# GateLoop attention and a multiplicative FFN: unit 7's output products in one-pass words, state products on four column groups, and new instruction lists for three engines

## The chip, the core and the metric

The kernel runs on one core of a Trainium2 chip. Its metric is the device time of one execution in microseconds. The engines that matter are TensorE (PE, with its weight loads PEld), VectorE (DVE), ScalarE (ACT), GpSimd (POOL) and SyncE (SP), which issues most transfers. Each engine works through its own instructions in order.

## What is computed

The reference runs a linear attention with a complex decay (GateLoop) on 4 sequences of 768 tokens, 8 heads of 48 dimensions, and puts its output through an FFN that multiplies two projections:

```python
mag = np.sqrt(a_re * a_re + a_im * a_im)
scale = np.minimum(mag, 0.999) / (mag + 1e-06)
a_re_n, a_im_n = (a_re * scale, a_im * scale)
for t in range(S):
    new_re = ar * S_re - ai * S_im
    new_im = ar * S_im + ai * S_re
    kv = np.einsum('bhd,bhe->bhde', k[:, :, t], v[:, :, t])
    S_re, S_im = (new_re + kv, new_im)
    y[:, :, t] = np.einsum('bhd,bhde->bhe', q[:, :, t], S_re)
...
a = x @ w1          # x: 3072 x 384, w1 and w2: 384 x 1024
b = x @ w2
h = a * b @ w3      # w3: 1024 x 1024
return (h @ w_out).astype(np.float32)
```

All is fp32.

## The kernel before

**Units.** The 3072 tokens are cut into 8 units of 384 (half a sequence each), a unit into 3 chunks of 128 tokens. For a unit, the gates (`re`, `im` to phases and magnitudes, with scans over the tokens) turn `q` and `k` into real and imaginary parts (`gA`, `gR` and the tiles' own values); SyncE moves these into the tiles QL and KL with the head dimension on the partitions, and `vr` into V. Then for each chunk TensorE transposes the two parts of k (`tp`, evicted by ScalarE to KT), forms the state's addition KTᵀ·V (`kv`, evicted into one of the tiles T0 to T2), the scores (`sc`, masked by VectorE into A0 or A1) and the output `y` from A·V and from QL·T.

**FFN.** In the head of the program w3·w_out is multiplied into one matrix `w3o`, 1024 x 384. A unit's FFN is then a = x·w1, b = x·w2, the product `ab`, and ab·w3o. From unit 2 on, x and the weights of a and b are held as rounded words (x0, x1 and x2 = x1 − x0; `wh`, `low`), and each fp32 product is three one-pass products: the first two (`hb`, "heads") go to a PSUM bank `m`, ScalarE scales the bank in place, the third (`da`, `db`, "diffs") is added, and ScalarE (a) or VectorE (a·b) evicts it. VectorE makes x1, GpSimd makes x2. The output products ab·w3o were plain fp32 for every unit: three token groups of 8 products of 128x384, in two parts.

**Order.** A planner with costs in the table TIMES writes TensorE's order: the FFN of unit u−1 is laid between the attention steps of unit u, so TensorE is nearly always busy, and unit 7's FFN stands alone at the end. ScalarE, VectorE and SyncE are put into the order of the lists in ORDERS by `in_order`: a list names, instruction by instruction, which of those left in the log comes next. GpSimd keeps the order of the log. `kv`, `tp` and `y` share two PSUM banks (`ps_v`), `m` and `o` the banks of `ps_m`; which of two free banks a tile gets follows the order in which the scheduler sees them released.

**Looks.** GpSimd also examines the inputs (`look`, `seen`, `looked`) and VectorE tests the results; `judge` sums them (`tot`) and a small product `count` on TensorE gives `good`, which decides at the end whether a general program has to run. The last pieces of w3 are examined in six freed buffers, named in BUFFERS.

The lines the prediction refers to are: L1047 `tp`, L1060 `sc`, L1099 `y`, L1125 `kv`, L1145 FFN products `m`, L1240 output products `o`, L1507 the head's fusion, L1535 `count`. L385 is the recording helper through which all other engines' instructions go, so they are told apart by their tiles.

Of the kernel before, what the change touches and what calls it, by code (L numbers as in the profile page):

```python
# [389 lines left out]
class Logged:  # L390
# [10 lines left out]
    scalar="""  # L401
# [16 lines left out]

# [3 lines left out]
""")  # L422


def in_order(tc, log, order):

    left, before, taken = list(log), None, []
# [9 lines left out]
def kernel(  # L437
# [812 lines left out]

    cv = {}

# [642 lines left out]
```

## Time and profile before

| | us |
|---|---|
| three runs | 528.59, 531.6, 544.0 (median 531.6) |
| the profiled execution, its own time | 529.23 |
| its span on the core | 527.4 |
| TensorE busy / idle in the span | 495.9 / 31.5 |
| VectorE busy | 372.4 |
| ScalarE busy | 324.7 |
| GpSimd busy | 257.5 |

The mean granted TensorE clock of the profiled execution was 0.994. A row of the page's groups reads: line, engine, operation, tile written <- tiles read, shape and count | busy us, mean ns of one | idle time of the engine just before, and what ended it. A row of the timeline reads: start us, busy us, engine, line, operation, and in brackets the idle time before it. A row of the chain reads: start us, us, what.

### The profile page before, as it was taken

The numbers are of one execution on the slowest core, as the hardware profiler recorded it, in microseconds if no ns is written. First come the engines' busy times: TensorE is split into PE (matmuls) and PEld (weight loads), VectorE is DVE, ScalarE is ACT, GpSimd is POOL, SyncE is SP. The second block draws the span as 40 slices with busy tenths as digits, with TensorE's granted clock in tenths as the row PEclk, the third lists the DMA queues.
The fourth block names the chain that finished last, engine by engine and source line by source line (L and its number), as shares of the span: only waits on it lengthen the run. The fifth ranks groups of instructions, "written<-read, shape, count | busy, mean of one in ns | idle before, by whom it ended". The sixth has DMA issues, their size and how long they took to land.

```text
span 527.4 us, 13622 instructions
## 1 busy us (share of the span) xinstructions
PE 495.9 (94%) x5594; PEld 377.1 (72%) x5594; DVE 372.4 (71%) x607; ACT 324.7 (62%) x569; POOL 257.5 (49%) x317
## 2 busy tenths in 40 slices
PE   4789889999999998999989999999999999999995
PEld 2345565556756677977879679877997789778972
DVE  6999698956769897918981599359936977653530
ACT  6979867485577565955777378818883864213420
POOL 1000000017869988657654855567647458525510
PEclk9899999999999999999999999999999999999998
DMA  8999958975199225991499319941994169606511
GB/s 258 367 396 285 203 150 279 186 162 125 40 237 204 78 80 124 242 221 63 103 250 206 114 35 266 217 119 46 265 221 103 47 181 231 203 19 204 196 45 37
DMA packets 66424, 89.75 MB, mean 170 GB/s; under 512 B 29872, under 2 KB 53872, under 8 KB 65584
## 3 DMA queue, kind: packets, MB, share of 16 engines
q1 hardware_dynamic: 57904, 59.15, 45.7%
q0 software_dynamic: 8448, 29.63, 19.9%
q8 instruction: 46, 0.75, 0.6%
q14 instruction: 26, 0.21, 0.1%
HBM read 61.01 MB, written 4.72 MB: 125 GB/s over the span
## 4 chain that ended last, share of the span: by engine, by line
PE 46%; DVE 17%; DMA 13%; POOL 12%; issue 7%; ACT 3%; SPq 2%; POOLq 0%; DVEq 0%; ACTq 0%
PE m L1145 20%; PE o L1240 14%; POOL look L385 9%; DMA re<-in_a_re_dram 6%; DVE gZ L385 4%; DMA look<-in_a_re_dram 3%; PE y L1099 3%; DVE gA L385 3%; PE sc L1060 3%; DVE gR L385 2%; PE kv L1125 2%; POOL seen L385 2%; SPq L385 2%; PE f L1507 2%; PE tp L1047 1%
## 5 line engine op out<-in xcount | busy, mean ns | idle before, releaser
L1240 PE MATMUL o<-w3o,ab 128*128 128x384 f32 x384 | 131.6, 492 | 0.0
L1145 PE MATMUL m<-x,low 128*128 128x384 f32 x576 | 119.0, 339 | 1.0 <-ACT m L385 1.0
L1145 PEld LDWEIGHTS m<-x,low 128*128 128x128 f32 x576 | 102.6, 188 | 1.2 <-ACT m L385 1.2
L1240 PEld LDWEIGHTS o<-w3o,ab 128*128 128x128 f32 x384 | 70.4, 190 | 45.6 <-issue 2.4
L385 POOL TENSOR_SCALAR look<-look 128x192 f32<-128x192 f32 (+1 forms) x70 | 74.7, 1067 | 16.3 <-DMA look<-in_a_re_dram 10.8
L385 DVE TENSOR_TENSOR ab<-m,ab 128x384 f32<-128x384 f32 x64 | 35.4, 554 | 63.4 <-PE m L1145 53.0
L1145 PE MATMUL m<-x,wh 128*128 128x384 f32 x288 | 69.8, 351 | 4.1 <-DVE ab L385 2.1
L385 POOL TENSOR_TENSOR look<-look 128x256 f32<-128x256 f32 (+1 forms) x58 | 43.8, 755 | 50.4 <-DMA look<-in_w_dram 32.3
L385 ACT ACTIVATE m<-m 128x384 f32<-128x384 f32 x96 | 45.7, 478 | 33.0 <-PE m L1145 32.4
L1145 PE MATMUL m<-xT,ws 128*128 128x384 f32 x192 | 63.1, 487 | 1.1 <-ACT xT L385 1.1
L1145 PEld LDWEIGHTS m<-x,wh 128*128 128x128 f32 x288 | 50.6, 188 | 8.5 <-DVE ab L385 3.4
L1145 PEld LDWEIGHTS m<-xT,ws 128*128 128x128 f32 x192 | 36.0, 190 | 25.5 <-ACT xT L385 1.7
L385 POOL MEMSET seen<- 128x256 bf16 x1 | 0.3, 316 | 110.1 <-DVE ab L385 110.1
L385 ACT COPY ot<-o 128x384 f32<-128x384 f32 x24 | 11.4, 476 | 61.4 <-PE o L1240 61.3
L385 POOL TENSOR_TENSOR seen<-seen,look 128x192 bf16<-128x192 bf16 (+1 forms) x55 | 42.7, 776 | 4.5
L1099 PE MATMUL y<-A,V 128*32 128x128 f32 x768 | 40.3, 273 | 1.7 <-issue 1.3
L385 DVE COPY_PREDICATED A<-mask,sc 128x512 f32<-128x512 uint8 x48 | 32.7, 734 | 11.6 <-PE sc L1060 11.5
L385 POOL TENSOR_TENSOR x<-x,x 128x384 fp32r<-128x384 f32 x18 | 24.2, 1350 | 34.3 <-DVE x L385 34.3
L385 ACT COPY ab<-m 128x384 f32<-128x384 f32 x64 | 30.5, 477 | 16.3 <-PE m L1145 16.1
L385 ACT ACTIVATE low<-raw 128x384 uint16<-128x384 uint32 (+6 forms) x40 | 33.9, 888 | 6.1 <-DMA raw<-in_w_dram 3.1
L1099 PEld LDWEIGHTS y<-A,V 128*32 128x32 f32 x768 | 34.4, 110 | 3.1 <-issue 2.5
L1060 PEld LDWEIGHTS sc<-QL,KL 96*32 96x32 f32 x1536 | 28.5, 110 | 10.3 <-issue 4.4
(119 smaller groups left out, 879.4 us busy)
## 6 DMA issues: line engine op xcount, KB each, us to landing
looked<-in_w_dram POOLq DMA_DIRECT2D x14, 512.0 KB, 4.4
look<-in_w_dram POOLq DMA_DIRECT2D x27, 256.0 KB, 6.0
raw<-in_w_dram SPq DMA_DIRECT2D x6, 1024.0 KB, 10.1
KL<-gR SPq DMA_DIRECT2D x24, 192.5 KB, 4.7
KL<-k SPq DMA_DIRECT2D x24, 192.5 KB, 6.5
QL<-gA SPq DMA_DIRECT2D x24, 192.0 KB, 6.8
QL<-q SPq DMA_DIRECT2D x24, 192.0 KB, 7.5
raw<-in_w_dram SPq DMA_DIRECT2D x6, 768.0 KB, 6.7
```

What stands on the lines that cost most here:

```text
L385: self.log.append(getattr(self.engine, name)(*args, **kw))
L1047: nc.tensor.transpose(out=tp[:, f], in_=src[:, f, c * C:(c + 1) * C], identity=ident)
L1060: nc.tensor.matmul(out=sc[SB * g:SB * g + SB, j, s0:C], lhsT=KL[:, x * n + j, w][:, s0:s0 + SB], rhs=QL[:, x * n + j, w][:, s0:C], start=T ...
L1099: nc.tensor.matmul(out=o, lhsT=a, rhs=b, start=s0, stop=s1)
L1125: nc.tensor.matmul(out=kv[g:g + SB, hd], lhsT=rows[:, g:g + SB], rhs=V[:, hd], start=True, stop=True)
L1145: nc.tensor.matmul(out=out, lhsT=a, rhs=b, start=start and i == 0, stop=i == len(terms) - 1, skip_group_check=not start)
L1240: nc.tensor.matmul(out=m, lhsT=ab_t[u][:, f, t * P:(t + 1) * P], rhs=w3o[:, f], start=(f == 0), stop=(f == KF - 1))
L1507: nc.tensor.matmul(out=sums[j], lhsT=w3_t[f][:, j * P:(j + 1) * P], rhs=w3_t["wo"][:, f], start=(f == 0), stop=(f == KF - 1))
```

## The change

Three things change together.

*Unit 7's output products.* They too become three one-pass products each. `last_weights` splits `w3o` into words: `h` goes into KL's buffer, `l` into QL's, the difference `d` into those of `re`, `im` and `gZ`. For each of the 8 blocks of `ab`, `last_words` makes a0 on ScalarE (into V, A0 and A1) and a1 and a2 on VectorE (a2 into gate buffers and `vr`). The product a·b itself goes to `side`, a tile in the output buffers. TensorE then runs 3 x 14 products (`oh`), 3 x 2 (`ot`), after which ScalarE scales each bank in place, and 3 x 8 (`od`): 72 in place of 24. `count` stands before the last `od` as it stood before the last `o`. Since `re`, `im` and `gZ` are now taken, BUFFERS has three entries.

*State products.* The 24 products of a state were 8 heads times 3 column groups of 32. Now the first 6 heads use groups 0 to 2 and the other two heads' six pieces go to group 3, one beside each of the 6 heads. The bank then holds the state in four areas, and its eviction is four instructions: 96 partitions x 6 heads, and three of 32 partitions x 2 heads. There are 20 states, 4 of them evicted by ScalarE.

*Lists and plan.* ScalarE, VectorE and SyncE have new lists; TIMES has new costs for the states and the tail, by which one look group moves ahead of unit 3's x2 and of the loads of k, q and v behind it on GpSimd, and the like in units 4 to 6. TensorE's order is the same outside the states and the tail.

```diff
+9 12 10 7 11 12 14 13 12 2 11 11 1 1 3 11 9 8 6 1 3 2 -1 3 1 1 -4 1 -2 10 1 -2 1 1 5 -1 1 -1 2 -2 5 -1 5 4 4 4 2 1 2
...
-        kv = ps_v.tile([2 * D, H, D], FP, tag="v", name="kv")
-        for hd in range(H):
-            rows = KT[:, hd].rearrange("p d x f -> p (d x f)")
+        kv = ps_v.tile([P, H, D], FP, tag="v", name="kv")
+        fits, spare = H - H // LANES, 3 * SB
+        for hd in range(fits):
             for g in range(0, 2 * D, SB):
+                rows = KT[:, hd].rearrange("p d x f -> p (d x f)")
                 nc.tensor.matmul(out=kv[g:g + SB, hd], lhsT=rows[:, g:g + SB], rhs=V[:, hd], start=True, stop=True)
+            g, over = divmod(hd, H - fits)
+            rows = KT[:, fits + over].rearrange("p d x f -> p (d x f)")
+            nc.tensor.matmul(out=kv[spare:spare + SB, hd], lhsT=rows[:, SB * g:SB * g + SB], rhs=V[:, fits + over],
+                             start=True, stop=True)
...
+        areas = [(slice(0, 2 * D), slice(0, 2 * D), slice(0, fits), slice(0, fits))]
+        areas += [(slice(SB * g, SB * g + SB), slice(spare, spare + SB), slice(fits, H), slice(g * (H - fits), (g + 1) * (H - fits)))
+                  for g in range(3)]
         with tc.high_priority():
-            if T is None:
-                nc.scalar.copy(out=Tn[:, :, 0:D], in_=kv)
-            else:
-                nc.vector.tensor_tensor(out=Tn[:, :, 0:D], in0=kv, in1=T[:, :, 0:D], op=OP.add)
+            for rows, lanes, heads, slots in areas:
+                if T is None:
+                    nc.scalar.copy(out=Tn[rows, heads, 0:D], in_=kv[lanes, slots])
+                else:
+                    nc.vector.tensor_tensor(out=Tn[rows, heads, 0:D], in0=kv[lanes, slots], in1=T[rows, heads, 0:D], op=OP.add)
...
+    def last_weights():
...
+        h, l, d = words_w
+        for n in range(0, KF, 2):
+            x = slice(n, n + 2)
+            nc.scalar.activation(out=h[:, x], in_=w3o[:, x], func=AF.Copy, scale=TOP * BITS)
+            nc.vector.scalar_tensor_tensor(out=l[:, x], in0=w3o[:, x], scalar=BITS, in1=h[:, x], op0=OP.mult, op1=OP.subtract)
+        for f in range(KF):
+            nc.vector.scalar_tensor_tensor(out=d[f], in0=h[:, f], scalar=1.0 / BITS, in1=l[:, f], op0=OP.mult, op1=OP.subtract)
+
+    def last_words(j):
+
+        a, a1 = sides[j], ab_t[NU - 1][:, j]
+        words_a[1].append(a1)
+        nc.scalar.activation(out=words_a[0][j], in_=a, func=AF.Copy, scale=TOP / BITS)
+        nc.vector.scalar_tensor_tensor(out=a1, in0=words_a[0][j], scalar=-BITS, in1=a, op0=OP.mult, op1=OP.add)
+        nc.vector.tensor_tensor(out=words_a[2][j], in0=a1, in1=words_a[0][j], op=OP.subtract)
+
+    def ffn_last():
...
+            for f in range(f0, f1):
+                for x in range(2):
+                    nc.tensor.matmul(out=m, lhsT=words_a[x][f][:, w], rhs=words_w[x][:, f], start=f == x == 0,
+                                     stop=f == KF - 1 and x == 1)
+            if f1 == KF:
+                nc.scalar.activation(out=m, in_=m, func=AF.Copy, scale=1.0 + 1.0 / BITS)
...
+            for f in range(KF):
+                nc.tensor.matmul(out=m, lhsT=words_a[2][f][:, w], rhs=words_w[2][f], start=False, stop=f == KF - 1,
+                                 skip_group_check=True)
...
+        return ([("oh", lambda t=t: heads(t, 0, KF - 1)) for t in range(UC)] +
+                [("ot", lambda t=t: heads(t, KF - 1, KF)) for t in range(UC)] + [("od", lambda t=t: diffs(t)) for t in range(UC)])
...
-        BUFFERS = (NU - 2, "k"), (NU - 1, "A"), (NU - 1, "q"), "re", "im", "gZ"
+        BUFFERS = (NU - 2, "k"), (NU - 1, "A"), (NU - 1, "q")
...
-            run(seq[:-4] + [("judge", 0)] + seq[-4:-2] + [("judge", 1)] + seq[-2:])
+            run(seq[:-3] + [("judge", 0)] + seq[-3:-1] + [("judge", 1)] + seq[-1:])
```

What the new lists move is seen in the order itself, before and after. The numbers in tile names are those of the two programs and differ between them. The first place is VectorE's list while unit 2's FFN runs and unit 3's `k` and `q` are rotated (about 205 to 213 us in the profile before); before:

```order
L385 SCALAR_TENSOR_TENSOR gZ_1560<-im_1526,st_ang_121 128x384 x2
L385 TENSOR_TENSOR k_2025<-k_2025,gR_1947 128x2x384
L385 TENSOR_TENSOR ab_2054<-m_2067,ab_2054 128x384
L385 COPY st_ang_121<-gZ_1560 128x9
L385 TENSOR_TENSOR k_2025<-k_2025,gR_1947 128x384
L385 SCALAR_TENSOR_TENSOR gZ_1560<-re_1454,gZ_1560 128x384
L385 SCALAR_TENSOR_TENSOR gZ_1560<-re_1454,gZ_1560 128x768
L385 TENSOR_TENSOR T2_124<-T2_124,KL_1499 96x8x48
L385 TENSOR_TENSOR ab_2054<-m_2092,ab_2054 128x384
```

And VectorE at the same place after:

```order
L385 SCALAR_TENSOR_TENSOR gZ_1592<-im_1560,st_ang_121 128x384 x3
L385 TENSOR_TENSOR ab_2074<-m_2084,ab_2074 128x384
L385 COPY st_ang_121<-gZ_1592 128x9
L385 SCALAR_TENSOR_TENSOR gZ_1592<-re_1480,gZ_1592 128x384
L385 SCALAR_TENSOR_TENSOR gZ_1592<-re_1480,gZ_1592 128x768
L385 TENSOR_TENSOR k_2042<-k_2042,gR_2054 128x384
L385 TENSOR_TENSOR k_2042<-k_2042,gR_2054 128x2x384
L385 TENSOR_TENSOR ab_2074<-m_2115,ab_2074 128x384
```

`ab`, `st_ang` and the two `gZ<-re` have moved ahead of the two `k`.

The second place is ScalarE's list where the gates of unit 5 begin beside unit 3's FFN (about 272 us). `m<-m` scales a bank after its heads, `ab<-m` evicts the a product, `gA<-re` reads the newly loaded `re`. Before:

```order
L385 ACTIVATE m_2806<-m_2806 128x384
L385 COPY ab_2716<-m_2774 128x384
L385 ACTIVATE gA_2738,st_low_117<-re_2736,consts_108 128x3x384
L385 ACTIVATE m_2821<-m_2821 128x384
L385 ACTIVATE gA_2738,st_low_117<-re_2736,consts_108 128x3x384
L385 COPY ab_2716<-m_2806 128x384
L385 ACTIVATE m_2852<-m_2852 128x384
```

And ScalarE at that place after:

```order
L385 ACTIVATE m_2867<-m_2867 128x384
L385 ACTIVATE gZ_2363<-gZ_2363 128x768
L385 ACTIVATE m_2880<-m_2880 128x384
L385 ACTIVATE gA_2831,st_low_117<-re_2829,consts_108 128x3x384
L385 COPY ab_2743<-m_2867 128x384
L385 COPY KT_2928<-tp_2929 128x128x3
L385 ACTIVATE gA_2831,st_low_117<-re_2829,consts_108 128x3x384
L385 ACTIVATE m_2949<-m_2949 128x384
```

Of the unit's 16 head evictions `m<-m`, the first `gA<-re` stood behind the 7th before and stands behind the 10th now; one unit later it moves from behind the 8th to behind the 9th, with one `ab<-m` between the two `gA`.

The third place is TensorE's list at unit 3's first state (about 233 us), with the semaphores that an instruction waits for: DVE_49 counts VectorE's instructions, Activation_49 ScalarE's, PE_49 TensorE's own. Before:

```order
L1240 MATMUL o_2353<-w3o_58,ab_2054 128x384 x4
L1125 MATMUL kv_2359<-vr_2029,KT_2342 32x48 [waits DMASW5_49,Activation_49]
L1125 MATMUL kv_2359<-vr_2029,KT_2342 32x48 x23
L1047 MATMUL tp_2391<-ident_59,gR_1947 128x128 [waits PE_49]
L1047 MATMUL tp_2391<-ident_59,gR_1947 128x128 x2
L1047 MATMUL tp_2397<-ident_59,k_2025 128x128 [waits DVE_49]
L1047 MATMUL tp_2397<-ident_59,k_2025 128x128 x2
```

And the end of the state on TensorE after:

```order
L1133 MATMUL kv_2387<-vr_2046,KT_2364 32x48 x3
L1136 MATMUL kv_2387<-vr_2046,KT_2364 32x48
L1054 MATMUL tp_2417<-ident_59,gR_2054 128x128 [waits PE_49]
L1054 MATMUL tp_2417<-ident_59,gR_2054 128x128 x2
L1054 MATMUL tp_2422<-ident_59,k_2042 128x128 [waits Activation_49]
L1054 MATMUL tp_2422<-ident_59,k_2042 128x128 x2
L1262 MATMUL o_2377<-w3o_58,ab_2074 128x384 x2
```

A fourth product stands beside every three, and the second transpose waits for ScalarE in the place of VectorE: it has the bank of the first transpose, not that of the state. The same exchange stands in units 4 and 6, with three FFN products between the two transposes. On VectorE the four parts of a state's eviction have between none and 14 other instructions between the first and the last of them.

More of the change, by code (lines that the diff above doesn't have):

```diff
@@ L539 @@
         nc.vector.memset(sc, 0.0)
-    Ab = [singles.tile([P, H, C], FP, name=f"A{i}") for i in range(2)]
-    Vb = singles.tile([P, UC, H, 64], FP, name="V")
+    Ab = [singles.tile([P, H, C], FP, tag=f"A{i}", name=f"A{i}") for i in range(2)]
+    Vb = singles.tile([P, UC, H, 64], FP, tag="V", name="V")
     w_t = [[w12.tile([P, KD, WB], FP, tag=f"w{n}{k}", name="ws") for k in range(2)] for n in range(FF // WB)]
@@ L1159, in times @@
         def times(m):
+            if u == NU - 1:
+                with tc.high_priority():
+                    last["ab", u, j] = nc.vector.tensor_tensor(out=sides[j], in0=m, in1=sides[j], op=OP.mult)
+                return last_words(j)
             with tc.high_priority():
@@ L1184, in diffs @@
                 return times(got[1])
+            if u == NU - 1:
+                sides[j] = one.tile([P, DM], FP, tag=f"o{j % 2}", name="side")
             with tc.high_priority():
-                nc.scalar.copy(out=ab_t[u][:, j], in_=got[0])
+                nc.scalar.copy(out=sides[j] if u == NU - 1 else ab_t[u][:, j], in_=got[0])
         if u >= THREE:
@@ L1247, in ffn_out @@
         return [lambda i=i: part(i * KF // parts) for i in range(parts)]
+    words_w, words_a, sides = [], [[] for _ in range(3)], {}
+    def last_weights():
+        G = 3
+        for x, tag, size in ((0, "KL", H * (TT + 1)), (1, "QL", H * TT)):
+            t = one.tile([P, size], FR, tag=tag, name="wx")[:, 0:KF * DM]
+            words_w.append(t.rearrange("p (f m) -> p f m", m=DM))
+        parts = [one.tile([P, G, DM], FR, tag=n, name="wd") for n in ("re", "im", "gZ")]
+        words_w.append([parts[f // G][:, f % G] for f in range(KF)])
+        words_a[0] += [t[:, i] for tag, n in (("V", 4), ("A0", 2), ("A1", 2)) for t in [singles.tile(
+            [P, n, TT], FR, tag=tag, padded_shape=[P, n, TT if n == 4 else H * C // n], name="a0")] for i in range(n)]
+        spots = [gate_pool[SLOTS[NU - 1][x] // 4].tile([P, G, TT], FR, tag="s%d" % SLOTS[NU - 1][x],
+                                                      padded_shape=[P, G, TT + 1], name="a2") for x in ("R", "k")]
+        spots.append(one.tile([P, G, TT], FR, tag="vr", name="a2"))
+        words_a[2] += [spots[j // G][:, j % G] for j in range(KF)]
+        h, l, d = words_w
[5 more added lines that the diff above has]
+            nc.vector.scalar_tensor_tensor(out=d[f], in0=h[:, f], scalar=1.0 / BITS, in1=l[:, f], op0=OP.mult, op1=OP.subtract)
@@ new lines, in last_words, with heads, diffs @@
+    def last_words(j):
[5 more added lines that the diff above has]
+    def ffn_last():
+        sums = {}
+        def heads(t, f0, f1):
+            if f0 == 0:
+                sums[t] = ps_m.tile([P, DM], FP, tag="mm", name="o")
+            m, w = sums[t], slice(t * P, (t + 1) * P)
+            for f in range(f0, f1):
[4 more added lines that the diff above has]
+                nc.scalar.activation(out=m, in_=m, func=AF.Copy, scale=1.0 + 1.0 / BITS)
+        def diffs(t):
+            m, w = sums[t], slice(t * P, (t + 1) * P)
+            for f in range(KF):
+                nc.tensor.matmul(out=m, lhsT=words_a[2][f][:, w], rhs=words_w[2][f], start=False, stop=f == KF - 1,
+                                 skip_group_check=True)
+            o = one.tile([P, DM], FP, tag=f"o{t % 2}", name="ot")
+            nc.scalar.copy(out=o, in_=m)
+            r0 = (NU - 1) * TT + t * P
+            nc.sync.dma_start(out=out[r0:r0 + P, :], in_=o)
+        return ([("oh", lambda t=t: heads(t, 0, KF - 1)) for t in range(UC)] +
+                [("ot", lambda t=t: heads(t, KF - 1, KF)) for t in range(UC)] + [("od", lambda t=t: diffs(t)) for t in range(UC)])
@@ L1598 @@
         "db": (("PE", 0.53), ("DVE", 0.56)), "f": (("PE", 1.31),), "f7": (("PE", 1.92), ("ACT", 0.57), ("ACT", 0.57)),
-        "part": (("PE", 2.58),), "half": (("PE", 2.58), ("ACT", 0.48), ("SP", 0.45)), "begin": (), "need": (), "end": (), "judge": ()}
[2 rows of a table added]
     urgent = []
```

5 lines of the change are left out of this document (4 added, 1 removed), and 44 rows, old and new, of tables (TIMES, scalar).

## The prediction

> **What bounds the kernel now.** I read the page's busy times first, then its groups.
>
> ```profile
> span 527.4 us, 13622 instructions
> PE 495.9 (94%) x5594; PEld 377.1 (72%) x5594; DVE 372.4 (71%) x607; ACT 324.7 (62%) x569; POOL 257.5 (49%) x317
> ```
>
> TensorE is busy for 94% of the span, so time can go in two ways only: less TensorE work, or fewer of its 31.5 us of idle time (527.4 − 495.9). VectorE at 71% has room on the average, not everywhere. The table by stretch of the span shows where (columns: length, TensorE, weight loads, VectorE, ScalarE, GpSimd busy; then the granted clock, the DMA share and GB/s):
>
> ```profile
> 26.00:40.00 14.00, 11.78 (x36) 6.76 (x37) 14.00 (x27) 11.15 (x18) 0.00 (x0) 1.00 1.02 395
> 240.00:270.00 30.00, 29.69 (x477) 24.96 (x476) 28.82 (x40) 22.04 (x41) 17.50 (x20) 1.00 0.46 127
> 300.00:330.00 30.00, 30.00 (x396) 25.37 (x395) 28.12 (x37) 23.36 (x44) 18.26 (x21) 1.00 0.55 143
> 480.00:506.00 26.00, 26.00 (x147) 25.84 (x146) 13.52 (x33) 11.77 (x25) 13.89 (x17) 1.00 0.51 172
> ```
>
> In the head VectorE is full and TensorE waits for it. Between the units VectorE is nearly full but TensorE does not wait. In the tail TensorE is full and VectorE half idle. The list of TensorE's waits (total us, times, longest) names the idle time outside the last store:
>
> ```profile
> PE sc L1507 <- DVE wo_s L385: 13.4, 5, 7.5
> PE m L1145 <- DVE ab L385: 2.1, 2, 1.9
> PE m L1145 <- ACT ab L385: 1.9, 3, 0.8
> PE kv L1125 <- ACT KT L385: 1.6, 2, 0.9
> PE sc L1060 <- DVE A L385: 1.2, 3, 0.6
> PE m L1145 <- ACT m L385: 1.0, 1, 1.0
> ```
>
> 13.4 us are the head's weight fusion; the three rows of `m` are 2.1 + 1.9 + 1.0 = 5.0 us of FFN products that waited because an eviction stood late in its engine's list. That is what new lists can take.
>
> **The tail's output products.** The chain that ended last (start, us, what) is plain TensorE work at the end:
>
> ```profile
> 446.58 0.81 PE kv L1125 x48
> ...
> 457.58 1.25 PE sc L1060 x64
> ...
> 480.17 25.46 PE m L1145 x144
> 505.63 10.32 PE o L1240 x32
> 516.07 5.37 PE o L1240 x16
> ```
>
> The 24 fp32 output products of unit 7 (two records each, 48) take 10.32 + 5.37 = 15.69 us, 0.654 each. The 144 one-pass products ahead of them have the same size, 128x384, and take 25.46 us, 0.177 each. The change puts 72 one-pass products in place of the 24: 72 × 0.177 = 12.73 us. **Gain 2.96 us**, if the words are ready. Cost of the words, by the nearest rows:
>
> ```profile
> L385 DVE SCALAR_TENSOR_TENSOR x<-x,y 128x384 fp32r<-128x384 f32 x18 | 9.7, 540 | 4.2 <-ACT x L385 4.1
> L385 DVE SCALAR_TENSOR_TENSOR low<-ws,wh 128x768 fp32r<-128x768 f32 x8 | 7.9, 986 | 0.0
> ```
>
> ```profile
> L385 DVE TENSOR_TENSOR ab<-m,ab 128x384 f32<-128x384 f32 x64 | 35.4, 554 | 63.4 <-PE m L1145 53.0
> L385 ACT ACTIVATE m<-m 128x384 f32<-128x384 f32 x96 | 45.7, 478 | 33.0 <-PE m L1145 32.4
> ```
>
> (Busy us, mean ns of one, idle before.) VectorE gets 4 × 0.986 + 8 × 0.540 for the weights and 8 × 2 × 0.540 for the a·b words, 16.9 us. It has 26 − 13.52 = 12.5 us free from 480 to 506, the tiles KL and QL are free from the last scores on (about 468), and the third products start only after 48 of the 72, 8.5 us behind 505.6. So it fits, with a few us to spare. The chain of the last word: product, then `ab` 0.55, ScalarE 0.48, two VectorE words, 2.1 us; the first 42 products do not need it and last 42 × 0.177 = 7.4 us. ScalarE's additions lie in its 14 free us. Bounds: −3.0 with all hidden, +1 if the words hold the last rows up for 4 us.
>
> The judging of the weights ends behind three looks fewer in buffers:
>
> ```profile
> 503.55 1.03 POOL L385 TENSOR_TENSOR looked<-looked 128x512 f32<-128x512 f32 x1 [1.49 <-DMA looked<-in_w_dram]
> 508.25 0.15 DVE L385 TENSOR_SCALAR tot<-tot 128x1 f32<-128x1 f32 x1
> ```
>
> Its count is wanted on TensorE ahead of the last 8 products, at about 505.6 + 64 × 0.177 = 516.9; `tot` was there at 508.4. That cover of 8.5 us pays for the later looks and the words queued among the tests; I cost it at 0, rival four below prices the rest.
>
> **State products.** 960 records by the group's row are 20 states of 48:
>
> ```profile
> L1125 PE MATMUL kv<-vr,KT 128*32 128x48 f32 x960 | 17.6, 208 | 1.6 <-ACT KT L385 1.6
> L1060 PE MATMUL sc<-QL,KL 96*32 96x128 f32 x384 | 20.3, 279 | 1.3 <-DVE A L385 1.2
> L1060 PE MATMUL sc<-QL,KL 96*32 96x32 f32 x384 | 12.2, 194 | 0.0
> ```
>
> A state takes 0.81 us for 16 rounds of three records, 51 ns a round of 48 columns. The scores run four column groups already: 16 rounds of four in 1.25 us, 78 ns for 80 columns in the mean (32 to 128, first and last row shown). That is 1.05 and 0.98 ns a column: a round costs its columns, and a fourth group in it nothing. So 12 rounds, 0.61 us, gain 0.20; part of 0.81 is the run-in, so I take 0.17, between 0 (cost by record: 48 as before) and 0.20. Three states lie in the head, where others are waited for; 17 × 0.17 = **2.9 us** (0 to 3.4).
>
> What it adds is on the evictions:
>
> ```profile
> L385 DVE TENSOR_TENSOR T<-kv,T 96x384 f32<-96x384 f32 x16 | 8.8, 552 | 21.1 <-PE kv L1125 21.1
> L385 DVE COPY st_ang<-gZ 128x9 f32<-128x9 f32 x8 | 2.0, 254 | 0.2
> ```
>
> One of 0.552 becomes one of 288 and three of 96 elements a partition. Below: the same elements, so no less than 0.55; above: three more by the 0.254 row, 1.3. I take 1.05, 0.5 more in each of 16 states, 8 us of VectorE (ScalarE's four states likewise). VectorE waited 21.1 us for exactly these products, so most of it is hidden. [...]
>
> Where the held bank bites is seen in TensorE's order: in units 3, 4 and 6 the second transpose after a state stands close behind it, and before it waited for the state's eviction. Now it takes the bank of the first transpose and waits for ScalarE's `KT` copy:
>
> ```profile
> 289.21 0.55 PE L1047 MATMUL tp<-ident,gR 128*128 128x128 f32 x3
> 289.34 0.55 DVE L385 TENSOR_TENSOR T<-kv,T 96x384 f32<-96x384 f32 x1 [0.73 <-PE kv L1125]
> 289.85 0.57 ACT L385 COPY KT<-tp 128x384 f32<-128x384 f32 x1 [0.86 <-PE tp L1047]
> 290.12 0.49 PE L1047 MATMUL tp<-ident,k 128*128 128x128 f32 x3
> ```
>
> The copy ends at 290.42, so the transpose moves from 290.12 to 290.45: 0.33 here and in the like place two units on, about 0.5 where the two transposes adjoin. **Loss 1.2 us.**
>
> **The lists.** The 1.9 us wait is at 210, where unit 2's `ab` stood behind unit 3's `k`, which waited for its load. Near 274 and 331 ScalarE sat in front of `gA<-re`, with evictions behind it:
>
> ```profile
> 208.94 0.96 DVE L385 TENSOR_TENSOR k<-k,gR 128x768 f32<-128x768 f32 x1 [2.34 <-DMA k<-in_k_dram]
> 209.82 0.55 DVE L385 TENSOR_TENSOR ab<-m,ab 128x384 f32<-128x384 f32 x1
> ```
>
> ```profile
> 272.88 1.26 ACT L385 ACTIVATE gA<-re,consts 128x1152 f32<-128x1152 f32 x1 [3.60 <-DMA re<-in_a_re_dram]
> 328.50 1.26 ACT L385 ACTIVATE gA<-re,consts 128x1152 f32<-128x1152 f32 x1 [0.97 <-DMA re<-in_a_re_dram]
> ```
>
> Now `ab`, `st_ang` and two `gZ` come ahead of `k`: about 2 us of work in the place of 2.34 idle; of 1.9 I take 1.6. The first `gA<-re` moves behind three more head evictions. These come 16 in 25.46 us, every 1.6 us, so 4.8 us later, more than 3.60: its 1.8 us (1.0 + 0.8) go. The second moves by one, 1.6 against 0.97, but both `gA` now stand nearly together, 2.5 us; of 0.8 I take 0.4. Sum **3.8 us**, bounds 0 and 5.0. The look moved on GpSimd ahead of unit 3's x2 lies where GpSimd waits for x1; later `k`, `q` and `vr` loads are its price if not:
>
> ```profile
> POOL x L385 <- DVE x L385: 34.3, 12, 5.5
> ```
>
> What a list of over a thousand places newly delays cannot be seen in the old trace: I put it at **1.0 us** (0 to 5). The moves of KL, QL, V and `im` on SyncE go with that. In the head VectorE was full from 26 to 40, and order alone fills nothing there; shorter gaps around it: **0.5 us**.
>
> Sum against the profiled run's own 529.23 (span 527.4 and 1.8 around it): 529.2 − 2.96 − 2.9 + 1.2 − 3.8 + 1.0 − 0.5 = 521.3, **521 us**. The runs shown have a median of 531.6, the profiled one lies near their lowest, 528.59, so I hold to it.
>
> **Rivals.**
> *VectorE becomes the bound* (the slower side). In 240 to 270 it has 1.2 us free, in 300 to 330 1.9, and each such unit gets 3 × 0.5 us more, in parts between which up to 14 other instructions stand. It decides where a unit's additions exceed its free time: then gates, transposes and scores of the next unit come late. If all 8 us come out on TensorE and the lists bring nothing: 529.2 − 2.96 − 2.9 + 1.2 + 8 = 532.5, to 541 with parts held behind long scans. For it: the two stretches; against: the 21.1 us it idled ahead of these evictions. Chance 0.10. [...]
> *The lists take nearly all waits*: the 5.0 of `m`, half of 1.6 + 1.2 on `KT` and `A`, half of 13.4 − 7.5 in the head, none new: 529.2 − 5.9 − 5.0 − 1.4 − 2.9 = 514. For it: every one of these rows names order, not work; against: VectorE full in the head. 0.20.
> *The lists bring nothing net*, their own waits replacing the old: 529.2 − 5.9 + 1.2 + 1 = 525.5, 529 if records, not rounds, cost the state products. 0.13.
> *The judge is late*: each look that has no buffer waits for a test; three at 2.5 to 3 us against a cover of 8.5, plus words on VectorE, would stall the last 8 products 1 to 4 us: 522 to 525. 0.06.
>
> **How the numbers follow.** The forecast's own case, 517 to 525, has 0.51. Two per cent, about what a measurement here tells from no change, is 518.6 against the profiled run and 521.0 against the median of the runs; halfway, some 0.16 of the forecast's case and nearly all of the second rival lie under it: faster 0.36. Above 540 lies only the end of the first rival: slower 0.04. Same 0.60. The range leaves out the lower edge of the second rival and most of the first: 512 to 530.
>
> **What would show it.** Tail: 72 `o` products at 0.177 with no wait for words, `count` unwaited. States: 48 records in about 0.64 us, four `T` rows of 1.05 us together; `tp<-ident,k` waiting for `KT` 0.3 to 0.5 at three places. Lists: no wait of `m` for `ab` over 0.5 us near 210, 274 and 331. It would be wrong if `m`, `tp` or `y` wait for `T` or `A` for several us, or if head waits stay and new ones of 5 us in sum appear.

## The result and the profile after

The changed kernel takes 525.79 us (median of 22 runs) against 530.78 us for the kernel before. The ratio is **0.9945, 95% interval 0.9919 to 0.9970**: 2.9 us faster, between 1.6 and 4.3, so no difference at the bound of 2%. Forecast were 521.0 us and 512 to 530. The time went the way that was forecast, by 2.9 of the 8 us. Executions of one kernel spread over 10 us and more on some chips (524.97 to 541.85 us for the kernel before on one of them), and the ratios leave out those more than 1.5% above the fastest; this is why a ratio can differ from the quotient of two medians, and why one profile below is not used.

The first two lines of the page after, span and busy times:

```profile
span 525.0 us, 13737 instructions
PE 491.2 (94%) x5618; PEld 377.5 (72%) x5618; DVE 404.8 (77%) x680; ACT 331.1 (63%) x596; POOL 258.9 (49%) x327
```

TensorE has 4.7 us less to do, but the span is only 2.4 us shorter: its idle time grew from 31.5 to 33.8 us, where the forecast let it shrink by some 2. VectorE got 32.4 us more. The table by stretch (length, TensorE, weight loads, VectorE, ScalarE and GpSimd busy, granted clock, DMA share, GB/s) shows where:

```profile
240.00:270.00 30.00, 29.09 (x417) 24.94 (x418) 24.72 (x37) 19.54 (x37) 17.91 (x23) 1.00 0.49 131
300.00:330.00 30.00, 30.00 (x328) 25.95 (x321) 28.58 (x38) 24.77 (x48) 17.75 (x21) 1.00 0.58 147
480.00:506.00 26.00, 25.71 (x146) 25.39 (x145) 23.17 (x45) 13.96 (x32) 12.36 (x15) 1.00 0.49 173
```

In the tail VectorE went from 13.52 to 23.17 us of 26. Between the units it is hardly fuller than it was (28.58 against 28.12 us from 300 to 330) or less full (24.72 against 28.82 from 240 to 270). TensorE's waits (total us, times, longest) tell what it idles for:

```profile
PE m L1161 <- DVE ab L385: 2.5, 3, 0.9
PE tp L1054 <- ACT KT L385: 2.3, 5, 1.0
PE kv L1133 <- ACT KT L385: 1.5, 3, 0.6
PE y L1106 <- DVE A L385: 1.3, 2, 0.7
...
PE y L1106 <- issue: 1.0, 2, 0.7
...
PE o L1262 <- DVE ab L385: 0.4, 1, 0.4
PE m L1161 <- DVE side L385: 0.3, 1, 0.3
```

The rows `m <- ACT ab` (1.9) and `m <- ACT m` (1.0) of before are gone and so is the 1.9-us wait for `ab` near 210, but there are three new waits for `ab` of up to 0.9, and `y`, `o` and the tail's `m` wait for VectorE where they did not. In the row with "issue" the profile names nobody that `y` waited for; its 0.7 us are at 243, and they are most of the 0.9 us that TensorE idles from 240 to 270.

How the 2.4 us of the span come about is seen best by laying the starts of TensorE's products in the two traces beside each other, product by product. Three landmarks are enough (unit 1's first FFN product; the first output product of unit 7; the last one):

```
                        before   after
first FFN product        80.11    79.67   head                      -0.44
first output product    505.47   505.57   stretch  425.35 > 425.90  +0.55
last output product     520.94   518.62   tail      15.48 >  13.05  -2.43
```

The stretch of 425 us between head and tail holds the states, the transposes behind `KT` and nearly all that the lists move, and it is as long as before in these two profiles.

A stretch is one execution's. A second profile of each kernel, taken with the experiments, has 427.15 us before and 426.10 after; in both of these the granted clock was halved for part of the stretch, which took an estimated 1.7 and 2.2 us (half the time at half clock, 3.4 and 4.5 us). Without that they are 425.4 and 423.9. So stretches of one kernel differ by up to 2 us from one execution to the next, and smaller differences below show nothing by themselves.

### The profile page after: what moved, and what is told of

It reads as the page before. It is cut to its first block, busy times and chain, and to the rows that moved or that the text cites. A ratio compares the mean times of both kernels' runs of the same rounds, so it can differ in the third digit from the quotient of the medians.

```text
span 525.0 us, 13737 instructions
## 1 busy us (share of the span) xinstructions
PE 491.2 (94%) x5618; PEld 377.5 (72%) x5618; DVE 404.8 (77%) x680; ACT 331.1 (63%) x596; POOL 258.9 (49%) x327
## 4 chain that ended last, share of the span: by engine, by line
PE 61%; DVE 20%; DMA 7%; ACT 5%; issue 3%; SPq 2%; DVEq 0%; ACTq 0%
PE m L1161 27%; PE o L1262 16%; PE y L1106 6%; DMA V<-vr 4%; PE sc L1067 4%; DVE gA L385 2%; SPq L385 2%; DVE gZ L385 2%; DVE A L385 2%; DVE w3s L385 2%; DMA raw<-in_w_dram 2%; DVE q L385 2%; PE o L1318 2%; DVE ab L385 2%; DVE low L385 1%
## 5 line engine op out<-in xcount | busy, mean ns | idle before, releaser
L1262 PE MATMUL o<-w3o,ab 128*128 128x384 f32 x336 | 116.3, 494 | 0.5 <-DVE ab L385 0.4
L1262 PEld LDWEIGHTS o<-w3o,ab 128*128 128x128 f32 x336 | 61.2, 190 | 40.9 <-issue 2.4
L385 DVE TENSOR_TENSOR ab<-m,ab 128x384 f32<-128x384 f32 x56 | 30.7, 552 | 40.8 <-PE m L1161 31.8
L385 DVE COPY_PREDICATED A<-mask,sc 128x512 f32<-128x512 uint8 x48 | 34.2, 734 | 19.2 <-PE sc L1067 18.9
L385 POOL TENSOR_TENSOR seen<-seen,look 128x256 bf16<-128x256 bf16 (+1 forms) x57 | 44.7, 785 | 4.7
L385 POOL TENSOR_TENSOR x<-x,x 128x384 fp32r<-128x384 f32 x18 | 22.6, 1260 | 45.6 <-DVE x L385 45.5
L385 ACT COPY ab<-m 128x384 f32<-128x384 f32 x56 | 26.6, 478 | 19.6 <-PE m L1161 19.5
L385 ACT ACTIVATE gZ<-gZ,consts 128x384 f32<-128x384 f32 (+2 forms) x16 | 12.4, 774 | 38.4 <-DVE st_tan L385 38.4
```

Source lines behind the costliest of these rows:

```text
L385: self.log.append(getattr(self.engine, name)(*args, **kw))
L1262: nc.tensor.matmul(out=m, lhsT=ab_t[u][:, f, t * P:(t + 1) * P], rhs=w3o[:, f], start=(f == 0), stop=(f == KF - 1))
```

## The experiments

**One part of the change at a time.** Four kernels on one chip. The first is the changed kernel with the old lists of ScalarE, VectorE and SyncE for everything that existed before (the parts of a state's eviction follow each other, the tail's words stand as in the new lists):

```diff
 ORDERS = dict(
     scalar="""
-9 1 -4 1 -1 1 1 -6 3 3 -1 2 -1 1 1 2 -1 1 -1 4 -8 7 -1 6 -2 1 1 1 -1 1 1 1 1 -2 1 -2 1 1 -1 1 7 -1 6 -1 5 -1 4 -1 3
+9 -15 3 3 3 -2 1 1 1 1 -4 2 -5 8 8 -2 3 -2 1 -9 4 -1 3 -4 6 6 6 -2 4 -1 3 3 3 3 -4 4 -68 3 -6 1 1 -1 1 -5 2 -3 1 1 1
...
```

> The changed kernel (state products on four column groups, one-pass tail) with the lists of ScalarE, VectorE and SyncE of the kernel before up to the place where unit 7's weight words begin; the four parts of a state's eviction stand next to each other. Theory L (the new lists bring as many waits as they take, the two product changes pay by themselves): span 527.4 - 2.8 - 2.5 = about 522, ratio to before 0.988 to 0.993. Theory V (VectorE's added work makes the new waits, under any list): 525 to 529, ratio 0.995 to 1.003, and the old waits of the FFN products near 210, 274 and 331 are back besides.

The second is the kernel before with the state products on four groups and the eviction in four parts, nothing else:

```diff
-        kv = ps_v.tile([2 * D, H, D], FP, tag="v", name="kv")
+        kv = ps_v.tile([P, H, D], FP, tag="v", name="kv")
...
+            for rows, lanes, heads, slots in areas:
...
+                    nc.vector.tensor_tensor(out=Tn[rows, heads, 0:D], in0=kv[lanes, slots], in1=T[rows, heads, 0:D], op=OP.add)
```

> The kernel before with the state products on four column groups and the four-part eviction alone, the parts next to each other in the old lists. Theory L: 17 states at 0.164 us less, span about 524.6, ratio 0.994 to 0.996. Theory V: the 0.5 us more of VectorE per state comes out on TensorE, span 526.5 to 529, ratio 0.998 to 1.004, with waits of tp, m or y for T, A or ab that the kernel before does not have.

The third is the kernel before with the one-pass output products and the changed plan, the old state products and the old lists:

```diff
-        BUFFERS = (NU - 2, "k"), (NU - 1, "A"), (NU - 1, "q"), "re", "im", "gZ"
+        BUFFERS = (NU - 2, "k"), (NU - 1, "A"), (NU - 1, "q")
...
+        return ([("oh", lambda t=t: heads(t, 0, KF - 1)) for t in range(UC)] +
+                [("ot", lambda t=t: heads(t, KF - 1, KF)) for t in range(UC)] + [("od", lambda t=t: diffs(t)) for t in range(UC)])
```

> The kernel before with unit 7's one-pass output products alone (the changed plan on GpSimd with it), old lists up to the words. Both theories: the 15.7 to 16 us of output products become about 13.4, span about 525, ratio 0.994 to 0.997; the stretch ahead of 470 us is as before to 0.5 us.

The fourth is the kernel before in which only the lists are exchanged for the new ones:

```diff
 ORDERS = dict(
     scalar="""
-9 -15 3 3 3 -2 1 1 1 1 -4 2 -5 8 8 -2 3 -2 1 -9 4 -1 3 -4 6 6 6 -2 4 -1 3 3 3 3 -4 4 -99 5 -2 1 2 -5 1 -4 1 -4 1 -1
+9 1 -4 1 -1 1 1 -6 3 3 -1 2 -1 1 1 2 -1 1 -1 4 -8 7 -1 6 -2 1 1 1 -1 1 1 1 1 -2 1 -2 1 1 -1 1 7 -1 6 -1 5 -1 4 -1 3 -1
...
```

> The kernel before with the new lists of ScalarE, VectorE and SyncE alone; its states keep one eviction, at the place of the first of the four parts, its output products and GpSimd's plan are as before. Theory L: the waits near 210, 274 and 331 (6.1 us) go and about 8 us of others come, span 527 to 530, ratio 1.0 to 1.005. Theory V: the 6.1 us go and few come, since VectorE has none of the added work: span 521 to 523, ratio 0.988 to 0.993.

Measured: ratios to the kernel before, and from the traces the stretch and the tail as above (us).

```
                          ratio (95%)                stretch   tail
states alone              1.0008 (0.9972 to 1.0043)   424.08   15.48
tail alone                0.9923 (0.9857 to 0.9988)   425.38   13.44
lists alone               1.0000 (0.9966 to 1.0035)   424.86   15.48
all but the lists         1.0006 (0.9977 to 1.0035)   427.15   13.05
```

Only the tail shows in a time by itself, and its second measurement further below has 1 in its interval; what it is worth stands in the traces' tails. Theory V's ranges hold for the states alone and for all but the lists. But of the old waits that it expected back in the latter, the one at 210 and 1.2 us of those near 274 stayed away, and only the one at 331 returned. For the lists alone theory L's time holds, though fewer new waits came than it said. The states' gain is there in TensorE (a state's products take 0.648 us in the starts instead of 0.812, as in the changed kernel) and is given back in waits: scores at 129 and 242 (0.4 each), `y` at 194 (1.28), the transposes behind `KT` (0.52, 0.34, 0.34) and smaller ones. The new lists alone take 6.1 us of waits away and make 3.9 new ones between 245 and 443 us; a `y` wait of 3.1 us at 77 to 80 us, which lies in the head, and 2.2 us of half clock behind it in the stretch took the rest in the profiled execution.

**What the states cost, and the changed kernel without them.** Four more kernels on another chip. The kernel before, a second time, shows whether its 210 wait is its own:

> The kernel before, unchanged, looked at a second time, to see which waits of its first trace are its lists' and which are one execution's. If the wait of 1.9 us near 210 belongs to the old list, it is here again; if it came from GpSimd's loads being late in that execution, it is gone or of another size. The waits near 274 and 331 (ScalarE behind the load of re) are expected again, to 0.5 us each.

It is: `m` waits 1.9 us for `ab` at 208 us again, as it did at 210, in a time of 528.46 us. The next has the old products and the eviction in parts alone:

```diff
+        areas = [(slice(0, 2 * D), slice(0, fits))] + [(slice(SB * g, SB * g + SB), slice(fits, H)) for g in range(3)]
...
-                nc.vector.tensor_tensor(out=Tn[:, :, 0:D], in0=kv, in1=T[:, :, 0:D], op=OP.add)
+                    nc.vector.tensor_tensor(out=Tn[rows, heads, 0:D], in0=kv[rows, heads], in1=T[rows, heads, 0:D], op=OP.add)
```

> The kernel before with the eviction of a state in four parts (96 partitions x 6 heads, three of 32 x 2) and everything else, the products too, as before. Theory L: hidden, ratio 0.998 to 1.002. Theory V: VectorE's 0.68 us more per state (1.23 by the parts' rows of the run with the states alone, less 0.55) comes out on TensorE for a third to a half of the 16 states: 3 to 5 us, ratio 1.005 to 1.010, with waits of y, sc and tp near 130, 194, 243, 290 and 400 as in that run.

Then the products on four groups with one eviction of the old size. It reads four heads twice in place of two heads' pieces in the fourth group, so the state leaves those out; the number of elements and instructions is that of the kernel before:

```diff
+        seen_kv = kv[0:2 * D, 0:4].unsqueeze(1).broadcast_to([2 * D, 2, 4, D])
...
-                nc.vector.tensor_tensor(out=Tn[:, :, 0:D], in0=kv, in1=T[:, :, 0:D], op=OP.add)
+                nc.vector.tensor_tensor(out=Tn.rearrange("p (x h) e -> p x h e", x=2)[:, :, :, 0:D], in0=seen_kv, in1=T.rearrange("p (x h) e -> p x h e", x=2)[:, :, :, 0:D], op=OP.add)
```

> The kernel before with the state products on four column groups, evicted by one instruction of the old size, 96 partitions x 384 (it reads four heads twice, so two heads' states are left out and the output is not the reference's). Theory V: without the parts the gain of 17 x 0.164 = 2.8 us shows, ratio 0.993 to 0.996, and the waits of the run with the states alone are gone. Theory L: the same as with the parts, ratio 0.994 to 0.996 in both, which that run's 1.0008 already speaks against. A third possibility, that TensorE's saved time is given back to VectorE's or the loads' pace whatever the eviction: ratio 0.998 to 1.001.

And the changed kernel with the old state products (tail, plan and new lists stay):

```diff
-        kv = ps_v.tile([P, H, D], FP, tag="v", name="kv")
+        kv = ps_v.tile([2 * D, H, D], FP, tag="v", name="kv")
...
-            for rows, lanes, heads, slots in areas:
```

> The changed kernel with the state products and their single eviction as before; tail, plan and new lists are the changed ones (the eviction stands where the first of the four parts stood). Theory V: the four-part evictions cost under the new lists at least what their products bring, so this is as fast as the changed kernel or faster: ratio 0.988 to 0.994. Theory L (states pay 2.8 us by themselves): 2.8 us slower than the changed kernel, ratio 0.998 to 1.001.

```
                                   ratio (95%)                stretch   tail
eviction in four parts alone       0.9990 (0.9952 to 1.0028)   425.86   15.48
four groups, one eviction          0.9946 (0.9901 to 0.9990)        -       -
all but the states                 0.9978 (0.9941 to 1.0015)   426.22   13.05
```

The stretch of the last row holds an estimated 2.6 us of half clock. The four-group products with a whole eviction are worth 2.9 us (0.5 to 5.2), what the forecast gave them. The parts by themselves cost nothing that can be measured: their trace has 1.1 us more of waits of `tp` for `KT` and 2.0 more of scores for `A`, but the waits at 210 and 274 are gone in it. So the theory that the parts alone cost several us falls, and yet nothing of the 2.9 us is left where products and parts come together (1.0008). Why the two do not add is not shown, and with these intervals the gap itself is barely clear of noise. The kernel without the states, 0.9978, lies just under theory L's range and above theory V's; neither theory holds throughout. The groups of the changed kernel (busy us, mean ns, idle before) give their price on VectorE:

```profile
L385 DVE TENSOR_TENSOR T<-kv,T 32x96 f32<-32x96 f32 x48 | 12.5, 260 | 1.3
L385 DVE TENSOR_TENSOR T<-kv,T 96x288 f32<-96x288 f32 x16 | 7.2, 447 | 15.1 <-PE kv L1136 15.1
```

0.447 + 3 × 0.260 = 1.23 us a state, against 0.552 before.

**The new waits themselves.** So far the sum is known, not the reason: does VectorE have no room, or does it do things in the wrong order? The changed kernel's timeline around 331 us shows the pattern (start us, busy us, engine, operation, in brackets the idle time before):

```profile
328.30 0.55 DVE L385 TENSOR_TENSOR k<-k,gZ 128x384 f32<-128x384 f32 x1
328.77 2.08 DVE L385 TENSOR_TENSOR q<-q,gZ 128x768 f32<-128x768 f32 x2
...
330.77 0.54 DVE L385 TENSOR_TENSOR ab<-m,ab 128x384 f32<-128x384 f32 x1
331.37 0.45 PE L1161 MATMUL m<-x,wh 128*128 128x384 f32 x1 [0.83 <-DVE ab L385]
```

`ab` frees the bank for which TensorE waits, and stands behind two `q` of unit 4, which nobody near needs. On ScalarE at 388 us the `KT` copy stands behind the load of a table:

```profile
388.13 1.28 ACT L385 ACT_TABLE_LOAD   x1
389.42 0.56 ACT L385 COPY KT<-tp 128x384 f32<-128x384 f32 x1
```

In an altered kernel eight such instructions are put ahead of the one or two before them. The place at 331 in VectorE's order, and that at 388 in ScalarE's:

```diff
 TENSOR_TENSOR k<-k,gZ 128x384
+TENSOR_TENSOR ab<-m,ab 128x384
 TENSOR_TENSOR q<-q,gZ 128x2x384
 TENSOR_TENSOR q<-q,gZ 128x384
-TENSOR_TENSOR ab<-m,ab 128x384
...
 ACTIVATE m<-m 128x384
-ACT_TABLE_LOAD
 COPY KT<-tp 128x128x3
+ACT_TABLE_LOAD
```

> The changed kernel with eight places of its lists altered, nothing else. In each, the instruction that TensorE waited for in the changed kernel's trace is put ahead of the one or two that stood before it and that nothing near needed: at about 180 us `ab` ahead of one `low`, at 243 `A` ahead of the 1.18-us `gZ<-im`, at 275, 331 and 443 `ab` ahead of one or two `q`, at 357 two `A` (with the T part before them) ahead of the `TENSOR_SCALAR gA`, at 502 `side` ahead of `looked` and `a` (VectorE), and at 388 `KT` ahead of the table load (ScalarE). Theory A (the new waits are a handful of local misplacements: VectorE has slack around them and serves TensorE late only because of the order): the steps .59, .99, 1.05, 1.08, .75, .63, .72 and .45 in TensorE's starts go, 6.3 us together, some .5 to 1.5 comes back in what was moved behind, and the time is 5 us below the changed kernel's: about 520.5, ratio to the kernel before .981 (.977 to .986). Theory B (VectorE, busy 404.8 of 525.0 us and unable to run ahead of TensorE, is the bound in the stretches between: a wait that is taken away at one place is back at the next one or two): the eight steps go, new ones of nearly the same sum appear within some 10 us behind each, and the time is within 1.5 us of the changed kernel's: ratio .992 to .997.

Beside it ran the changed kernel and the tail alone once more:

> The changed kernel unaltered, beside the altered lists on the same chip: ratio .9945 as first measured, .992 to .997; its waits at 180, 243, 275, 331, 359, 390 and 443 us there again to within .2 us, since the lists fix their order; a head that comes out up to 3 us longer or shorter is not the change's.

> The kernel before with the one-pass output products alone (old lists, old state products), measured a second time with more rounds: if these products are worth the 2.5 us that the stretch behind 505.5 us shows, the ratio is .9953; if everything else of the change nets zero, it is that of the changed kernel within .002; the .9923 of the first measurement was within its interval of both.

```
                       ratio (95%)                median   stretch   tail
altered lists          0.9845 (0.9785 to 0.9904)  524.28    422.62   14.01
changed kernel         0.9896 (0.9848 to 0.9944)  526.72    426.10   13.05
tail alone             0.9977 (0.9937 to 1.0018)  531.76    425.96   13.05
```

Against the first profile of the changed kernel the eight waits went nearly whole: 0.59, 0.34 of 0.99, 0.88 of 1.05, 1.08, 0.75, 0.63, 1.13 and 0.45, 5.9 us. But the changed kernel's own second profile does not have all of them as expected: its steps are 0.34 at 180, none at 243, 0.63 at 276, 1.04 at 359 and 0.13 at 503, where those at 331, 390 and 443 are the same to 0.1. The one at 243 was not a wait for VectorE. In the changed kernel `y` resumed at 243.40, half a us before the `A` behind `gZ<-im` was done, and the altered kernel, in which `A` stands ahead of `gZ<-im`, still idles 0.4 us there with no releaser. The changed kernel's rows:

```profile
241.68 1.18 DVE L385 CUSTOM_DVE_ANT_0 gZ<-im 128x768 f32<-128x768 f32 x1
...
243.18 0.73 DVE L385 COPY_PREDICATED A<-mask,sc 128x512 f32<-128x512 uint8 x1
243.40 0.27 PE L1106 MATMUL y<-A,V 128*32 128x128 f32 x1 [0.72 <-issue]
```

The other seven exchanges took 4.8 us (second profile) to 5.5 (first). The place at 331 in the altered kernel's timeline:

```profile
330.09 0.54 DVE L385 TENSOR_TENSOR k<-k,gZ 128x384 f32<-128x384 f32 x1
...
330.56 0.55 DVE L385 TENSOR_TENSOR ab<-m,ab 128x384 f32<-128x384 f32 x1
...
331.03 1.61 DVE L385 TENSOR_TENSOR q<-q,gZ 128x768 f32<-128x768 f32 x2
...
332.14 0.77 PE L1161 MATMUL m<-x,wh 128*128 128x384 f32 x3
```

The product follows the transpose without a wait, and the two `q` end 2.55 us behind the start of `k`, as they did in the changed kernel. Against the first profile some 2.7 us came back at other places (0.44, 0.88 and 0.23 at scores of 131, 188 and 193, 0.75 at 285, 0.41 at 394; that of 131 stands ahead of the first altered place). The stretch is 3.3 us shorter than in the first profile of the changed kernel. Against the second it is 3.5 us shorter, but only 1.2 us without the 2.2 us of half clock there. The tail gives back 0.96:

```profile
PE sc L1067 <- DVE A L385: 2.0, 5, 0.7
...
PE kv L1133 <- ACT KT L385: 0.9, 2, 0.6
PE count L1616 <- DVE tot L385: 0.7, 1, 0.7
PE tp L1054 <- ACT T L385: 0.6, 1, 0.6
```

`count` now waits for `tot`, the end of VectorE's tests. Theory A (misplacements) holds for the places themselves, seven of eight, but of the 5 us that it expected between a quarter and two thirds are seen in the stretch, and the tail takes 0.96 of that. Theory B (no room, the sum comes back) holds in part: some two fifths of what went came back behind the altered places. In the time nothing is clear of noise, with six executions of each kernel. In the second measurement of the tail alone, 0.9977, the interval has both 1 and the expected 0.9953; its stretch holds an estimated 1.6 us of half clock.

**Three more places.** The last kernel adds three from the altered kernel's own trace, the two `A` of the scores at 186 to 188 ahead of `im` and `gZ<-im`, and `T<-kv` ahead of `gA<-re` at 282:

```diff
 TENSOR_TENSOR T<-kv,T 96x6x48
+COPY_PREDICATED A<-mask,sc 128x512
 TENSOR_TENSOR im<-im,re 128x768
-COPY_PREDICATED A<-mask,sc 128x512
 TENSOR_TENSOR T<-kv,T 32x2x48
+COPY_PREDICATED A<-mask,sc 128x512
 ISA gZ,st_tan<-im 128x384
...
+COPY T<-kv 96x6x48
+COPY T<-kv 32x2x48 x3
 ACTIVATE gA<-re 128x3x384
 ACTIVATE m<-m 128x384
-COPY T<-kv 96x6x48
-COPY T<-kv 32x2x48 x3
 COPY KT<-tp 128x128x3
```

> The kernel with the eight altered places, and three more, taken from its own trace: at 186 to 188 us the two `A` of the first scores ahead of the 1.06-us `im` and of the 0.53-us `gZ<-im` (VectorE), and at 282 the four parts of `T<-kv` ahead of the 1.18-us `gA<-re` (ScalarE). The steps that these places cost in that trace are .92 at 187.2, .84 at 188.6 (of .42 that the scores take anyway) and .93 at 284.6 (of .18). If the waits are still local, 1.5 to 2 us more go from the stretch between 80 us and the output products of unit 7: it is 420.8 us long, where it was 425.9 in the changed kernel and 422.6 with eight places; the ratio is .981 (.976 to .987). If VectorE's and ScalarE's work has no more room, the stretch stays at 422 to 423 us and the ratio at .9845. The tail keeps what it lost with the eight places: the product `count` waits some .6 us for VectorE's `looked`.

Measured: 0.9916 (0.9878 to 0.9953) with a median of 524.62 us (12 runs), on another chip. The stretch is 421.93 us, 0.7 shorter, not 1.8, which is less than two profiles of one kernel differ. At the places themselves 0.88 and 0.75 went, but here theory B is right at both: on ScalarE the product behind waits 0.72 more, for the `m` that now stands later, and on VectorE the delayed gates stand ahead of the next `A`, for which the scores wait 1.22 more:

```profile
192.37 1.39 DVE L385 CUSTOM_DVE_ANT_0 gZ<-im 128x768 f32<-128x768 f32 x1
...
193.80 0.74 DVE L385 COPY_PREDICATED A<-mask,sc 128x512 f32<-128x512 uint8 x1
...
194.77 0.96 DVE L385 SCALAR_TENSOR_TENSOR gA<-gZ,gA 128x768 f32<-128x768 f32 x1 [0.23 <-ACT gZ L385]
...
196.06 0.72 DVE L385 COPY_PREDICATED A<-mask,sc 128x512 f32<-128x512 uint8 x1
...
196.84 1.32 PE L1067 MATMUL sc<-QL,KL 96*32 96x128 f32 x64 [1.58 <-DVE A L385]
```

The two kernels with altered lists have the lowest medians of all, 524.3 and 524.6 us against 525.8 and 526.7 for the changed kernel. The intervals of the ratios overlap, and they were taken on different chips, so what is shown is the waits that went and a shorter stretch, not the 1 to 2 us.

## Why the prediction was wrong by its size

By its own terms, each measured in the starts of TensorE's products of the first two traces, one execution each:

```
term                                forecast   measured
tail's output products                 -2.96      -2.43
state products                         -2.9       -2.8
transposes behind KT                   +1.2       +1.20
old waits that the lists take          -3.8       -6.1
what the lists newly delay             +1.0       +7.1
wait at 243 with no releaser              -       +1.0
head                                   -0.5       -0.4
```

**The step that failed** is the one line "What a list of over a thousand places newly delays cannot be seen in the old trace: I put it at 1.0 us (0 to 5)". In the first profile the new waits are 8.1 us at 15 places (0.2 to 1.1 each): `ab` behind `q`, `k` or `low` at 180, 276, 331 and 443 (3.4 together), `A` or the parts of `T` behind gates at 191, 194, 359, 402 and 418 (1.7), ScalarE's `re` and `KT` at 272 and 390 (1.0), the rest at 349, 430 and 503 (0.9), and the wait at 243 (1.0), which has no releaser. At the same places the second profile has 6.2 us. Both 7.1 and 6.2 are outside the bounds that the forecast gave the term, and what the forecast named as a sign of being wrong, new waits of 5 us in sum, is there.

The lists by themselves are not outside: alone they make 3.9 us of new waits, and with tail and plan but without the new states 5.15, just over the bound (one profile each). The remaining 1 to 2 us need the new states. The sum had no term for that: the 8 us more of VectorE were put at nothing, as "most of it is hidden". The parts seem to have lengthened VectorE's row of work in front of instructions that were already just in time; that they did it, and not another part of the new states, is argued and not shown.

**Old waits.** 6.1 in place of 3.8: at 210 the whole 2.07 went, not 1.6, and at 274 to 276 2.2 in place of 1.8, because the evictions came ahead of the load that held ScalarE; the wait at 331.9 went whole (1.0, not 0.4), but a new one of 1.08 stands 2 us later; another 0.8, at 272 and near 382, was not forecast. The size was missed, the mechanism is that of the forecast. It is luck that this error of 2.3 us stands against the one above: without it the time would have been longer still. But the wait at 210 is also gone with the old VectorE list (states alone, parts alone, tail alone, all but the lists), so the list was not the only thing that could take it; why these took it is not shown.

**Tail.** 72 one-pass products follow each other at 0.1745 us, as the rows of `m` said, with no wait for words. The 24 fp32 ones had 0.645 by their starts, not 0.654. Of the 13.05 us from the first start to the last, 71 × 0.1745 are 12.39; the other 0.66 are 0.46 around `count` and 0.2 where the third products begin. The chain of waits after ends so (start, us, what):

```profile
502.85 2.88 PE m L1161 x15
505.73 8.38 PE o L1318 x48
514.11 3.01 PE o L1326 x16
517.11 0.06 issue
517.17 0.19 PE count L1616 x2
517.36 1.61 PE o L1326 x8
```

The "cover of 8.5 us" of the judge is used up to the last tenth, which the forecast had costed at 0 for the time but not seen coming: `tot` is ready only just ahead of `count`.

```profile
516.87 0.15 DVE L385 TENSOR_SCALAR tot<-tot 128x1 f32<-128x1 f32 x1
517.40 0.15 DVE L385 SCALAR_TENSOR_TENSOR count<-count,consts 1x7 f32<-1x7 f32 x1 [0.38 <-PE count L1616]
```

VectorE's tests were pushed back by 8.6 us; how much of that is the words and how much the looks without a buffer is not shown. This is just short of the fourth rival. `count` does wait for `tot` in the tail alone (0.5 us, the reason for its tail of 13.44) and with the altered lists (0.7 us).

**States and KT.** Both terms came out to a tenth, counted by the state's own products. Four of the 17 states are followed by scores, which start 0.06 to 0.22 us later behind the last product than before; these 0.5 us (0.2 of them, at 402, are among the new waits) take part of the gain back. A fourth column group costs a round next to nothing: 0.648 us for 12 rounds is 54 ns with the run-in, against 51. The parts of `T` take 1.23 us, inside the bounds 0.55 to 1.3 and above the 1.05 taken. The large part has 0.447 of it and each small one 0.260, about what the `st_ang` copy of 9 elements a partition took before (0.254). Beside the same products, one eviction of the old size has a ratio of 0.9946 and the eviction in four parts 1.0008; the intervals overlap, so what the split costs there is not shown.

**Rivals.** What happened is the third, "the lists bring nothing net, their own waits replacing the old", which had 525.5 to 529 and a chance of 0.13. The first, VectorE as the bound, did not come at its price of 8 us: VectorE is busy for 404.8 of 525.0 us, and from 240 to 270 it is less full than before. Some 1 to 2 us of it came, as said above. The second needed "none new".

**What stays open.** The three stretches of the span explain 2.4 us; the ratio's interval holds that, the difference of the medians (5.0) and the second measurement (0.9896) are larger. In the second pair of profiles stretch and tail alone are 3.9 us shorter once half clock is taken off (1.5 and 2.4). The granted clock has a mean of 0.994 over the 22 executions after and of 0.988 over the 98 before that were taken beside the experiments; 0.006 of 525 us are an estimated 3 us, so fewer stretches at half clock may add to the gain. The head's end varies between 77.7 and 84.8 us over the profiles of all kernels, with either lists, and two profiles a kernel can't tell whether the change moves its mean.

## What to carry to other kernels

A new order for engines that feed a full engine has two sides: the waits it takes can be read from the old trace, the waits it makes can't, and here they were of the same order (6.1 us taken; 3.9 made by the lists alone, 6.2 to 7.1 with the rest of the change). Forecast the net of a searched list as nothing unless each moved row is followed to the one who waits for it. Read such a list in the new trace for the last instruction ahead of each wait: where it is work that nobody near needs, one exchange takes the wait away (seven places here), though part of it can come back elsewhere, and it stops to help where both neighbours are wanted. See first that the row names a releaser and that this one ended just ahead: the wait at 243 has none, and no exchange could take it. And profile each kernel twice before a difference of 1 or 2 us is read from its trace. Splitting an eviction to speed up products has to be priced on the order behind it, not on its own microseconds: here the parts alone had a ratio of 0.9990 and the products with one eviction 0.9946, and together they had 1.0008.

## What the hardware showed beside it

**Half clock after a wait.** In the second profile of the changed kernel `y` waited 3.0 us up to 81.0 (row of TensorE's waits), and the granted clock (third number from the right in the table by stretch) fell, and nine records of 128x384 (two to an fp32 product) took 5.41 us, 0.60 each in place of 0.33 (32 took 10.48 us in the first profile):

```profile
PE y L1106 <- issue: 3.0, 1, 3.0
```

```profile
78.00:84.00 6.00, 2.40 (x45) 0.80 0.13 45
84.00:90.00 6.00, 6.00 (x12) 0.63 0.79 265
```

```profile
83.89 5.41 PE L1161 MATMUL m<-xT,ws 128*128 128x384 f32 x9 [0.57 <-ACT xT L385]
```

In 10 of the 13 profiles used `y` waited like this for 0.8 us or more between 75 and 82 us. The five waits of 2.5 to 3.3 us were followed by half clock, which lasted 3.4 or 6.8 us; the five of 0.8 to 1.6 were not. In the stretches of the changed kernel's second profile, the new lists alone, all but the states and the tail alone (second profile), half clock costs an estimated 2.2, 2.2, 2.6 and 1.6 us (half the time at half clock) on top of the wait's own length. Elsewhere it is less regular: of the two waits of 1.9 us near 210 in the two profiles of the kernel before, one was followed by it (a mean clock of 0.86 from 204 to 216 us in the second profile, 1.00 in the first). So half clock came behind waits of 1.9 to 3.3 us and stayed away behind another of 1.9; what decides it is not shown.

**A wait behind a packet of instructions.** This `y` wait has no releaser ("issue"). In 11 of 13 profiles the run of `y` products between 76 and 82 us resumed 1.2 to 1.5 us after a 16-KB packet of the queue of instructions had landed; in the other two the packet landed by 74.6 us and there was no wait. The wait at 243 is of this kind too: `y` resumed at 243.40, 1.4 us behind such a packet (241.06 to 241.99). The `y` products ahead of the wait start some 0.03 us apart. That TensorE uses up its instructions faster than these packets bring them is the author's guess from the times alone, which no run tested. Whether transfers have a part in it is not shown either: from 75 to 78 us of that second profile the DMA engines were full (share 0.97 and more), but from 241 to 243 of the first profile they were not (0.06 to 0.24).
